# A nested seven-product scheme for the fourth product of stage one's first pair of steps, with a new order of stage one and S3 formed from S2

## The chip, the cores and the metric

The kernel runs on one core of one Trainium2 chip. The metric is the device time of one execution in microseconds; 904.12 us before the change, the median of three runs (904.05 to 904.26). The profile is that of one further execution.

## The reference

All data are fp32. An attention without softmax feeds a two-layer network:

```python
kv  = einsum('bhsd,bhse->bhde', k, v)      # 8 batches, 8 heads, 576 positions, head size 64
o   = einsum('bhsd,bhde->bhse', q, kv)
o   = o / sqrt(mean(o*o, -1) + 1e-6) * g_norm
x   = o with the heads side by side        # 4608 x 512
h   = x @ w_in                             # 512 x 2048
g   = s * relu(h)**2 + b
out = g @ w_out                            # 2048 x 512
```

## The kernel before

**Units and steps.** The 4608 rows of x are worked off in nine units (u = 0 to 8) of 512 rows. Each unit has a stage one (x times w_in, then relu, square and the affine of ScalarE) and a stage two (g times w_out). While unit u runs, the attention of unit u + 1 is done beside it, in two halves A and B: turn (VectorE L540, a transpose of q), product (TensorE L552), back (VectorE L564), square, row_sum (VectorE L575), norm (VectorE L585), turn_x (VectorE L592), scale. The k^T v products of the batches to come are kv (TensorE L384; ScalarE copies the result out at L400, into bd_kv).

**The seven-product scheme.** With C = A B in 2 x 2 blocks, seven products of half size take the place of eight: sums S1 to S4 of the one operand's blocks, sums T1 to T4 of the other's, products 1 to 7 of these, and sums of the products. Unit 0 is plain, unit 1 uses the scheme once, and units 2 to 8 use it on two levels: some of the seven products are themselves done by the scheme, with products of a quarter of their size.

**Stage one of units 2 to 8** (`mm1_deep`, L803 to L994). The 2048 columns of h are taken in four steps s = 0 to 3; steps 0 and 1 are pair 0, steps 2 and 3 pair 1. Here w_in is the operand A and x the operand B. Per step, products 1, 6, 5, 7 and 4 are whole products: `x1`, `x6`, `x5`, `y7`, `y4`, each a call of `mm1_product` with matmuls of 128x128 by 128x256. The function `y4(s)` multiplies A22 and T4 and adds the result to `r2`, kept in SBUF by `x6`. Products 2 and 3 go on by the scheme, for the two steps of a pair together: `small(i, pair, ...)` issues, for i = 2 or 3, small products 1 to 7 of 128x128 by 128x128 (four matmuls each), with their sums (`keep`, `add_relu`) on VectorE. The banks of PSUM for small are sx_ps (tag x of pool `ps_a`) for the small products 1, 6, 5 and 3, and z_ps (a single bank) for 2, 7 and 4. Of the sums of w_in that small needs, those of products 2 and 3 for both pairs (`DEEP`) are made once in unit 1 by `sums_of_w_in` and stored in DRAM (`w1_dram`) on the queue of POOL (GpSimd). SP loads them, like the parts of w_out, into a ring of NR = 14 slots (`pump` L1026), and a slot is freed by `used`. The sums of x for small are made by `sums_of_x` in `sub` tiles (six of them). Blocks of g are a11, a12, a21, a22 for each step, and s1 = a21 + a22; `done` does the square (L910) and the affine (L651) on ScalarE.

**Stage two of units 2 to 8** (`mm2`, `at_two_levels` L1110, `rest` L1368). g is A, w_out is B. All seven products go by the scheme, product 2 and 5 as one group, 7 and 3 as another. `do_25(6)` issues small product 6 of products 2 and 5; `go_73(1)` small product 1 of products 7 and 3, and `sums_...` forms the small sums of g on VectorE. S2, S3 and S4 of g are formed in place: `s2` writes S2 = S1 - A11 over a11, `s4` writes S4 = A12 - S2 over a12, and `s3` writes S3 = A11 - A21 over a21. Product 7 takes S3 as its operand. S3 of steps 0 and 1 is formed in stage one, the one just ahead of at(16), the other behind x5(3); S3 of steps 2 and 3 is formed in stage two, right after do_25(2) and at(1), by `step["s3"]`, before `s2` has overwritten a11.

**What sets the order.** The order is written out by hand: each engine carries out its own instructions in the order in which the functions are called, and there is no scheduler. In stage one `at(n)` calls the attention steps that `sides` (L1687) lists for the place n; stage two has places of its own. The lists for units 3 to 7 are the same but for kv, which stands at at(4) (at at(2) in unit 6) and is due in units 1 to 6; unit 2 has a list of its own, and unit 8 has none. The loads of q (L1624) and the stores of the output (L1211) go out on POOL's queue.

Of the kernel before, what the change touches and what calls it, by code (L numbers as in the profile page):

```python
# [10 lines left out]
FP32 = mybir.dt.float32  # L11
# [6 lines left out]
def kernel(  # L18
# [39 lines left out]
    nc = tc.nc  # L58
# [200 lines left out]
    def add(o, a, b):  # L259
        nc.vector.tensor_tensor(out=o, in0=a, in1=b, op=ALU.add)  # L260
# [53 lines left out]
    DEEP = ((2, 0), (3, 0), (2, 1), (3, 1))  # L314
# [464 lines left out]
    def sums_of_w_in(key, tags):  # L779

        i, pair = key
        w = [
            (ws[s][:, 2] if i == 3 else wa[s][:, KH:])
            for s in (2 * pair, 2 * pair + 1)
        ]
        a11, a12, a21, a22 = w[0][:, 0], w[0][:, 1], w[1][:, 0], w[1][:, 1]
        t = [
            xp.tile([P, KH, TB], FP32, name=f"xs_{n}", tag=f"xs_{n}").rearrange(
                "p k (b n) -> p (k b) n", n=P
            )  # L790
            for n in tags
        ]
        (s2, s3), (s1, s4) = ((x[:, :2], x[:, 2:]) for x in t)
        add(s1, a21, a22)
        sub(s2, s1, a11)
        sub(s3, a11, a21)
        sub(s4, a12, s2)
        for n in range(2):
            nc.gpsimd.dma_start(
                out=w1_dram[key][:, n], in_=t[n].rearrange("p f n -> p (f n)")  # L800
            )

    def mm1_deep(u):  # L803
# [4 lines left out]
        def sums_of_x():  # L808
            k0, k1 = (
                xT[u][:, KH + k].rearrange("p (g q c) -> p q g c", g=2, q=2) for k in range(2)  # L810
            )
            b11, b12, b21, b22 = k0[:, 0], k0[:, 1], k1[:, 0], k1[:, 1]
            t = [
                late["sub"].tile([P, FC // 4, P], FP32, name="sub", tag="sub", bufs=6) for _ in range(2)
            ]
            (t1, t2), (t3, t4) = ((x[:, :2], x[:, 2:]) for x in t)
            sub(t1, b12, b11)
            sub(t2, b22, t1)
            sub(t3, b22, b12)
            sub(t4, b21, t2)  # L820
            a.update({1: b11, 2: b21, 3: b22, 4: t4, 5: t1, 6: t2, 7: t3})
# [18 lines left out]

        def a22(s):
            t = g_tile("a22", s)
            add_relu(t, st["y", s], ga["a21", s])
# [10 lines left out]
        def s3(s):  # L854
            sub(ga["a21", s], ga["a11", s], ga["a21", s])

        def small(i, pair, *ms):
            name = {2: "a11", 3: "a21"}[i]

            def to(j, h):  # L860
                return g_pair[name, pair][:, j, :, h * P : h * P + P]

            def w_of(m):
                s0, s1 = 2 * pair, 2 * pair + 1
                raw = {1: (s0, 0), 2: (s0, 1), 4: (s1, 1)}
                if m in raw:
                    s, k = raw[m]
                    return ws[s][:, 2, k] if i == 3 else wa[s][:, KH + k]
                n, k = {6: (6, 0), 7: (6, 1), 5: (5, 0), 3: (5, 1)}[m]
                return ring[u, (i, pair), n][:, k]  # L870

            def keep(name, j, h):
                st[name] = late["tmp"].tile(
                    [P, 2, P], FP32, name="r", tag={"q2": "r2_2", "q4": "q4"}.get(name, "r14")
                )
                add(st[name], st["sx"], to(j, h))

            for m in ms:
                first = m in (1, 2, 7)
                if m == 1:  # L880
                    ps = ps_a.tile([P, DM], FP32, name="sx_ps", tag="x")
                    st["sx"] = ps.rearrange("p (b c) -> p b c", c=P)[:, :2]
                elif first:
                    ps = bank_of(("s", m), "z", 1).rearrange("p b (m c) -> p (b m) c", c=P)
                    st["sy"] = ps[:, :2]
                ps = st["sx" if m in (1, 6, 5, 3) else "sy"]
                w, x = w_of(m), a[m][:, i - 2]
                for b in range(2):
                    matmul(ps[:, b], w[:, b], x, first and b == 0, True)
                if m == 7:  # L890
                    used((u, (i, pair), 6))
                elif m == 3:
                    used((u, (i, pair), 5))
                if m == 1:
                    keep("q1", 0, 0)
                elif m == 2:
                    add_relu(to(0, 0), ps, st["q1"])
                elif m == 6:
                    keep("q2", 1, 0)
                elif m == 5:  # L900
                    keep("q4", 1, 1)
                    add_relu(to(1, 1), st["sy"], st["q4"])
                elif m == 3:
                    add_relu(to(0, 1), ps, to(0, 1))
                elif m == 4:
                    add_relu(to(1, 0), ps, st["q2"])
# [6 lines left out]
        def run(at, early):  # L913
# [6 lines left out]
            at(4)  # L920
            y7(0)
            small(2, 0, 6, 7)
            at(5)
            x5(0)
            small(2, 0, 5)
            a22(0)
            at(6)
            x6(1)
            done("a22", 0)
            small(2, 0, 3, 4)  # L930
            at(7)
            y4(0)
            at(8)
            y7(1)
            done("a11", 0, 1)
            at(9)
            x5(1)
            done("a12", 0)
            a22(1)
            at(10)  # L940
            x1(2)
            small(3, 0, 1, 2)
            at(11)
            x1(3)
            done("a22", 1)
            y4(1)
            at(12)
            small(3, 0, 6, 7)
            y7(2)
            at(13)  # L950
            small(3, 0, 5)
            x6(2)
            done("a12", 1)
            at(14)
            small(3, 0, 3, 4)
            x6(3)
            done("a21", 0)
            at(15)
            small(2, 1, 1, 2)
            x5(2)  # L960
            done("a21", 1)
            s1(0)
            s3(0)
            at(16)
            small(2, 1, 6, 7)
            a22(2)
            y7(3)
            done("a22", 2)
            s1(1)
            small(2, 1, 5)  # L970
            x5(3)
            s3(1)
            small(2, 1, 3, 4)
# [12 lines left out]
        def rest_of_3():  # L986
# [5 lines left out]
            s1=lambda: (s1(2), s1(3)), s3=lambda: (s3(2), s3(3)),  # L992
# [73 lines left out]
    def mm2(u, step=None, side={}):  # L1066
# [301 lines left out]
        def rest():  # L1368
# [21 lines left out]
            step["s3"]()  # L1390
# [21 lines left out]
            go_6(7)  # L1412
            do_6(5)
# [177 lines left out]
    def side_of(A, B, sums, u):  # L1591

        if u == 0:
# [9 lines left out]
        of_w_in = [  # L1603
            partial(sums_of_w_in, *with_tags)
            for with_tags in zip(DEEP, ((5, 6), (7, 4), (5, 6), (7, 4)))
        ]
# [5 lines left out]
            6: [B["norm"], of_w_in[1]],  # L1612
            8: [B["turn_x"], B["scale"], of_w_in[2]],
            9: [of_w_in[3]],
            11: [sums],
            13: [partial(loads, 3, 1)],
            3: [of_w_in[0]],
# [69 lines left out]
    def sides(u, A, B):  # L1687
# [9 lines left out]
        if u == 1:  # L1697
            for s in range(1, NS - 1):
                first[((0, 1), (0, 3))[s - 1]] = list(sums_w_in(s))
            first.update({  # L1700
                (1, 3): kv,
                (2, 0): [A["turn"]],
                (2, 1): [A["product"]],
                (2, 2): [A["back"]],
                (2, 3): [A["square"]],
                (3, 0): [A["row_sum"]],
                (3, 2): [A["norm"], A["turn_x"]],
                (3, 3): [lambda: [load() for load in load_q(12, rest_on=nc.sync)]],
            })
            return first, second  # L1710
        if u + 1 == U:
            return first, second
        if u == 2:
            first = {
                4: [A["turn"]],
                5: kv,
                8: [A["product"]],
                9: [A["back"], B["turn"]],
                10: [A["square"]],
                11: [A["row_sum"]],  # L1720
                12: [B["product"]],
                13: [A["norm"]],
                14: [A["turn_x"]],
                15: [B["back"], *q[0]],
            }
            second = {
                0: [B["square"]], 1: [B["row_sum"], A["scale"]], 2: [B["norm"]], 3: [B["turn_x"], *q[1]],
                "sums": [B["scale"]],
            }
        else:  # L1730
            first = {
                2: [A["turn"], *(kv if u == 6 else [])],
                4: [A["product"], *(kv if u != 6 else [])],
                5: [A["back"]],
                6: [A["square"], B["turn"]],
                7: [A["row_sum"]],
                8: [A["norm"]],
                9: [A["turn_x"]],
                10: [B["product"], *q[0]],
                11: [B["back"], A["scale"]],  # L1740
                12: [B["square"]],
                13: [B["row_sum"]],
                14: [B["norm"]],
                15: [B["turn_x"], *q[1]],
            }
            second = {1: [B["scale"]]}
# [101 lines left out]
```

## Time and profile before

| | |
|---|---|
| median of three runs | 904.12 us (904.05 to 904.26) |
| the profiled execution | 904.66 us |
| its span, from the first to the last instruction | 902.9 us |
| mean granted TensorE clock | 1.000 |
| instructions | 19433 |
| chain of work that ended last, by engine | PE 93%, VectorE 4%, DMA 1%, ScalarE 1% |
| the chain's largest lines | x_ps L92 46%, y_ps L92 28%, z_ps L92 10%, sx_ps L92 6% |
| starts of units 2, 3, 4, 5 (us) | 234.5, 332.2, 427.7, 523.6 |
| starts of units 6, 7, 8 (us) | 619.3, 715.2, 808.4 |

How to read it. Engines are PE (TensorE's matmuls), PEld (its weight loads, which overlap PE), DVE (VectorE), ACT (ScalarE), POOL (GpSimd), SP (SyncE, which issues loads). L92 is line 92 of the kernel; as all matmuls of this kind are issued by one helper there, and the additions and subtractions by the helpers at L260 and L263, they are told apart by their tiles: `z_ps<-sub,w_sb` is a matmul into the tile z_ps from the tiles sub and w_sb. A row of a timeline is the start in us from the beginning of the span, the length of the row in us, engine, line, operation, tiles, shapes, and the number of records that were drawn together (x8); in brackets stands the idle time of the engine just before it and what ended that. Matmuls are pipelined, so that rows of PE overlap, and the distance between two starts is the time that the first one took from the stream. A row of the waits is: the engine and the line that waited, the engine and the line that it waited for, then total us, number of times, and the longest.

### The profile page before, as it was taken

How to read it: one execution, taken by the hardware profiler on the slowest of the kernel's cores; microseconds unless marked ns; L12 is line 12 of the kernel's file. 1: busy time of each engine (PE TensorE's matmuls, PEld its weight loads, DVE VectorE, ACT ScalarE, POOL GpSimd, SP SyncE). 2: the span in 40 equal slices, each digit the busy share in tenths (PEclk: the TensorE clock that was granted, in tenths of full speed). 3: DMA queues.
4: the chain of work that ended last, by engine and by line, in shares of the span. 5: the costliest groups of instructions: out<-in, count | busy, mean ns of one | idle time of the engine just before them, and what ended most of it. 6: DMA issues, size and time to landing. Idle time of an engine off the chain costs nothing.

```text
span 902.9 us, 19433 instructions
## 1 busy us (share of the span) xinstructions
PE 891.4 (99%) x7578; PEld 822.1 (91%) x7578; DVE 658.2 (73%) x1240; ACT 347.0 (38%) x584; POOL 265.8 (29%) x501
## 2 busy tenths in 40 slices
PE   7999999999999999999999999999999999999998
PEld 6888888888889998999899988999899989999998
DVE  2898686687557975798668856885779767972696
ACT  2887023531157115720464026601670056204610
POOL 2027057014732333711373026503440300021000
PEclk9999999999999999999999999999999999999999
DMA  9897637249943994289527972599239812991286
GB/s 255 310 337 235 194 98 244 69 118 400 338 131 94 307 317 146 71 268 329 185 70 213 314 253 69 154 307 320 66 88 314 288 41 54 303 306 46 59 280 187
DMA packets 118987, 184.55 MB, mean 204 GB/s; under 512 B 25200, under 2 KB 42992, under 8 KB 118896
## 3 DMA queue, kind: packets, MB, share of 16 engines
q1 hardware_dynamic: 98288, 155.36, 54.0%
q0 software_dynamic: 17152, 25.72, 9.6%
q10 hardware_dynamic: 3456, 2.23, 1.0%
q8 instruction: 60, 0.98, 0.4%
q14 instruction: 31, 0.25, 0.1%
HBM read 157.03 MB, written 26.21 MB: 203 GB/s over the span
## 4 chain that ended last, share of the span: by engine, by line
PE 93%; DVE 4%; DMA 1%; ACT 1%; issue 0%; ACTq 0%; DVEq 0%
PE x_ps L92 46%; PE y_ps L92 28%; PE z_ps L92 10%; PE sx_ps L92 6%; PE y_ps L552 2%; DMA kv_sb<-in_v_dram 1%; PE kv_ps L384 1%; PE z_ps L384 1%; DVE a L263 0%; DVE xn L585 0%; PE y_ps L384 0%; DVE sub L263 0%; DVE xT L596 0%; DVE o L260 0%; DVE xs L263 0%
## 5 line engine op out<-in xcount | busy, mean ns | idle before, releaser
L1624 POOL DMA_DIRECT2D q_sb<-in_q_dram x312 | 175.8, 572 | 136.5 <-ACT a L910 76.2
L92 PE MATMUL x_ps<-w_sb,sub 128*128 128x128 f32 x1176 | 148.8, 275 | 1.1 <-DVE r L260 1.1
L1211 POOL DMA_DIRECT2D out_dram<-o x120 | 59.4, 502 | 303.8 <-issue 151.1
L92 PEld LDWEIGHTS x_ps<-w_sb,sub 128*128 128x128 f32 x1176 | 139.7, 192 | 1.5 <-DVE r L260 1.5
L651 ACT ACTIVATE a<-a,b_col,s_col 128x512 f32<-128x512 f32 x144 | 117.0, 813 | 26.1 <-DVE a L654 17.8
L92 PE MATMUL y_ps<-xs,wb 128*128 128x256 f32 x528 | 124.6, 381 | 0.0
L92 PEld LDWEIGHTS y_ps<-xs,wb 128*128 128x128 f32 x528 | 97.0, 190 | 12.9 <-issue 1.0
L826 ACT COPY a<-x_ps 128x512 f32<-128x512 f32 x28 | 16.3, 583 | 220.1 <-PE x_ps L92 220.1
L260 DVE TENSOR_TENSOR r<-sx_ps,a 128x256 f32<-128x256 f32 x84 | 35.4, 422 | 79.3 <-PE sx_ps L92 79.3
L92 PE MATMUL x_ps<-xs,ws_raw 128*128 128x256 f32 x384 | 91.2, 380 | 0.1
L92 PE MATMUL x_ps<-xT,wa 128*128 128x256 f32 x360 | 83.9, 381 | 0.1
L92 PEld LDWEIGHTS x_ps<-xs,ws_raw 128*128 128x128 f32 x384 | 70.0, 190 | 8.7 <-ACT r L725 0.5
L910 ACT ACTIVATE a<-a 128x512 f32<-128x512 f32 x112 | 69.8, 623 | 18.4 <-DVE a L267 18.4
L92 PEld LDWEIGHTS x_ps<-xT,wa 128*128 128x128 f32 x360 | 66.7, 190 | 10.4 <-issue 1.5
L92 PE MATMUL x_ps<-w_sb,a 128*128 128x128 f32 (+1 forms) x432 | 64.9, 298 | 0.0
L92 PE MATMUL y_ps<-w_sb,a 128*128 128x128 f32 (+1 forms) x416 | 62.1, 295 | 0.0
L92 PEld LDWEIGHTS x_ps<-w_sb,a 128*128 128x128 f32 x432 | 58.4, 192 | 2.9 <-issue 0.4
L92 PEld LDWEIGHTS y_ps<-w_sb,a 128*128 128x128 f32 x416 | 56.1, 192 | 2.1
L92 PE MATMUL y_ps<-w_sb,sub 128*128 128x128 f32 x392 | 49.5, 275 | 0.0
L260 DVE TENSOR_TENSOR r<-x_ps,o 128x256 f32<-128x256 f32 (+1 forms) x84 | 29.7, 353 | 26.7 <-PE x_ps L92 26.0
L263 DVE TENSOR_TENSOR a<-a,a 128x512 f32<-128x512 f32 x72 | 46.8, 684 | 0.4
L92 PE MATMUL z_ps<-w_sb,a 128*128 128x128 f32 (+1 forms) x352 | 46.9, 280 | 0.0
(207 smaller groups left out, 1512.1 us busy)
## 6 DMA issues: line engine op xcount, KB each, us to landing
w_sb<-w SPq DMA_DIRECT2D x399, 256.0 KB, 5.1
w_sb<-w SPq DMA_DIRECT2D x14, 512.0 KB, 8.8
w<-sub POOLq DMA_DIRECT2D x28, 256.0 KB, 6.6
out_dram<-o POOLq DMA_DIRECT2D x112, 64.0 KB, 4.1
w_sb<-in_k_dram SPq DMA_DIRECT2D x24, 288.0 KB, 4.8
w_sb<-in_v_dram SPq DMA_DIRECT2D x24, 288.0 KB, 5.0
w_raw<-in_moe_w_in_dram SPq DMA_DIRECT2D x6, 1024.0 KB, 8.1
q_sb<-in_q_dram POOLq DMA_DIRECT2D x160, 32.0 KB, 2.9
```

Source lines behind the costliest of these rows:

```text
L92: nc.tensor.matmul(o, lhsT=lhsT, rhs=rhs, start=start, stop=stop, skip_group_check=True)
L260: nc.vector.tensor_tensor(out=o, in0=a, in1=b, op=ALU.add)
L263: nc.vector.tensor_tensor(out=o, in0=a, in1=b, op=ALU.subtract)
L384: nc.tensor.matmul(ps[r][(r ^ l) * HB : (r ^ l) * HB + HB, i, :], lhsT=kv[l][0][rows, j, :], rhs=kv[l][1][rows, j, :], start=(j == 0), sto ...
L552: nc.tensor.matmul(ps[l][32 * p : 32 * p + 32, r, lo:hi], lhsT=bd_kv[b % 2][rows, p, at : at + 32], rhs=st["qT"][rows, p, lo:hi], start=Tr ...
L651: nc.scalar.activation(t, t, AF.Identity, scale=s_col, bias=b_col)
L826: nc.scalar.copy(g_tile("a11", s), st["x", s])
L910: nc.scalar.square(ga[name, s], ga[name, s])
L1211: queues[s % 2].dma_start(out=view[b, jj, :, cols], in_=st[name, j][s * w : s * w + w, cols])
L1624: load()
```

## The change

From unit 2 on, product 4 (A22 times T4) of steps 0 and 1 goes by the scheme too: `small(4, 0, ...)`, seven small products for the pair, takes the place of y4(0) and y4(1). Its result is accumulated in g's tile of a12, and `a12(s)` is y7's result plus r2 put there ahead of it, on VectorE. The sums of T4 are formed by `sums_of_x4` in one more `sub` tile (four subtractions of 128x128). The sums of w_in for the key (4, 0) are made, stored and loaded as for the others: two stores more in unit 1, and two loads of 256 KB more per unit. All these sums are now made in unit 1's stage one (before: in the stage two of that unit), in halves, in `sub` tiles.

As small(4, 0) and small(3, 0) run interleaved, as do small(3, 0) and small(2, 1), small(3, 0) gets banks of its own, from the pool `ps_t` (tag t, the one that the attention's transposes and products use), and tiles q1t, q2t, q4t of its own.

The order of stage one is new from the first y7 to the last x5. Among other things, small(2, 0, 6, 7) now stands ahead of y7(0) and right behind at(4) and at(5), and the places at(5) to at(16) lie elsewhere in the stream. The attention steps of `sides` are moved with it; in unit 2, whose attention ran into stage two, square and row_sum of B and scale of A are now in stage one.

S3 is now formed for all four steps at one place of stage two: after s4, do_6(2, 6) and go_6(7), and before do_6(5) and go_73(1), as a22 - a11, where a11 holds S2 by then.

```diff
-    DEEP = ((2, 0), (3, 0), (2, 1), (3, 1))
+    DEEP = ((2, 0), (4, 0), (3, 0), (2, 1), (3, 1))
...
-    def sums_of_w_in(key, tags):
+    def sums_of_w_in(key):
...
-        add(s1, a21, a22)
-        sub(s2, s1, a11)
-        sub(s3, a11, a21)
-        sub(s4, a12, s2)
-        for n in range(2):
-            nc.gpsimd.dma_start(
-                out=w1_dram[key][:, n], in_=t[n].rearrange("p f n -> p (f n)")
-            )
+        t = {}
+
+        def part(n, *steps):
+            x = late["sub"].tile([P, FC // 4, P], FP32, name="sub", tag="sub", bufs=6)
+            t[n] = x[:, :2], x[:, 2:]
+            for step in steps:
+                step()
+            nc.gpsimd.dma_start(
+                out=w1_dram[key][:, n], in_=x.rearrange("p f n -> p (f n)")
+            )
+
+        return (
+            lambda: part(0, lambda: sub(t[0][1], a11, a21), lambda: sub(t[0][0], a22, t[0][1])),
+            lambda: part(1, lambda: add(t[1][0], a21, a22), lambda: sub(t[1][1], a12, t[0][0])),
+        )
...
+        def sums_of_x4():
+            x = xs[u, 4]
+            b11, b12, b21, b22 = (x[:, k, q * P : q * P + P] for k in range(2) for q in range(2))
+            t = late["sub"].tile([P, FC // 4, P], FP32, name="sub", tag="sub", bufs=6)
+            t1, t2, t3, t4 = (t[:, n] for n in range(4))
+            sub(t1, b12, b11)
+            sub(t2, b22, t1)
+            sub(t3, b22, b12)
+            sub(t4, b21, t2)
...
+        def a12(s):
+            add(g_tile("a12", s), st["y", s], st["r2", s])
...
         def s3(s):
-            sub(ga["a21", s], ga["a11", s], ga["a21", s])
+            sub(ga["a21", s], ga["a22", s], ga["a11", s])
...
-            name = {2: "a11", 3: "a21"}[i]
+            name = {2: "a11", 3: "a21", 4: "a12"}[i]
+            g = (i, pair)
+            apart = g == (3, 0)
...
+            def bank_for(m):
+                if apart:
+                    ps = ps_t.tile([P, 2, 2 * P], FP32, name="st_ps", tag="t")
+                    return ps[:, 0].rearrange("p (b c) -> p b c", c=P)
+                if m == 1:
+                    ps = ps_a.tile([P, DM], FP32, name="sx_ps", tag="x")
+                    return ps.rearrange("p (b c) -> p b c", c=P)[:, :2]
+                ps = bank_of(("s", m), "z", 1).rearrange("p b (m c) -> p (b m) c", c=P)
+                return ps[:, :2]
```

The order in `run`, before and after (the calls of done left out, all others in their order):

```diff
-x1(0) at(2) x1(1) sums_of_x small(2,0,1,2) x6(0) at(4) y7(0) small(2,0,6,7) at(5)
-x5(0) small(2,0,5) a22(0) at(6) x6(1) small(2,0,3,4) at(7) y4(0) at(8) y7(1) at(9)
-x5(1) a22(1) at(10) x1(2) small(3,0,1,2) at(11) x1(3) y4(1) at(12)
-small(3,0,6,7) y7(2) at(13) small(3,0,5) x6(2) at(14) small(3,0,3,4) x6(3) at(15)
-small(2,1,1,2) x5(2) s1(0) s3(0) at(16) small(2,1,6,7) a22(2) y7(3) s1(1)
-small(2,1,5) x5(3) s3(1) small(2,1,3,4) a22(3) early at(18) y4(2) ...
+x1(0) at(2) x1(1) sums_of_x small(2,0,1,2) x6(0) at(4) at(5) small(2,0,6,7) y7(0) at(6)
+small(2,0,5) a12(0) x6(1) at(7) small(2,0,3,4) y7(1) sums_of_x4 a12(1) x5(0)
+small(4,0,1,2) a22(0) at(8) x5(1) small(4,0,6,7) at(9) a22(1) at(10) x1(2) at(11)
+small(4,0,5) x1(3) at(12) small(4,0,3,4) x6(2) at(13) small(3,0,1,2) y7(2) at(14)
+small(3,0,6,7) small(2,1,1,2) x6(3) at(15) small(3,0,5) small(2,1,6,7) x5(2)
+small(3,0,3,4) small(2,1,5) a22(2) y7(3) small(2,1,3,4) at(16) x5(3) s1(0) s1(1)
+a22(3) early at(18) y4(2) ...
```

Stage two, and the attention steps:

```diff
             do_25(2)
             at(1)
-            step["s3"]()
             s2((0,))
...
             s4((1, 2, 3))
             go_6(7)
+            step["s3"]()
             do_6(5)
             sums_73((5, 6), 7)
             sums_73((), 3)
             go_73(1)
...
         if u == 2:
-            first:  4 A.turn; 5 kv; 8 A.product; 9 A.back, B.turn; 10 A.square; 11 A.row_sum;
-                    12 B.product; 13 A.norm; 14 A.turn_x; 15 B.back, q[0]
-            second: 0 B.square; 1 B.row_sum, A.scale; 2 B.norm; 3 B.turn_x, q[1]; "sums" B.scale
+            first:  4 A.turn; 6 kv; 7 A.product; 8 A.back, A.square, B.turn; 9 A.row_sum;
+                    10 B.product; 11 B.back; 12 A.norm; 13 A.turn_x, q[0]; 14 B.square;
+                    15 B.row_sum; 16 A.scale
+            second: 1 B.norm; 2 B.turn_x; 3 q[1]; "sums" B.scale
         else:
-            first:  2 A.turn (kv, u == 6); 4 A.product (kv, u != 6); 5 A.back; 6 A.square, B.turn;
-                    7 A.row_sum; 8 A.norm; 9 A.turn_x; 10 B.product, q[0]; 11 B.back, A.scale;
-                    12 B.square; 13 B.row_sum; 14 B.norm; 15 B.turn_x, q[1]
+            first:  2 A.turn (kv, u == 5); 4 A.product (kv, u != 5); 5 A.back, A.square, B.turn;
+                    6 A.row_sum; 7 A.norm; 8 A.turn_x; 10 B.product, q[0];
+                    11 B.back, B.square, A.scale; 12 B.row_sum; 13 B.norm; 14 B.turn_x; 15 q[1]
```

In unit 1 the stage-two list loses its four calls of sums_of_w_in (places 3, 6, 8, 9), and the stage-one list gains ten halves, spread over the places (1, 0) to (3, 0) between the attention steps.

## The prediction, on record before the changed kernel ran

> **What bounds the kernel now.** I read the page first, then TensorE's waits, then the timelines of TensorE and VectorE (DVE) around the places that the diff touches. Units are counted from 0; unit 2 is the third.
>
> ```profile
> PE 891.4 (99%) x7578; PEld 822.1 (91%) x7578; DVE 658.2 (73%) x1240; ACT 347.0 (38%) x584; POOL 265.8 (29%) x501
> ```
>
> The waits of TensorE (engine, line, whom it waited for: total us, times, longest) hold only seven rows. Six belong to the start; the one below is all that it waits in the steady part:
>
> ```profile
> PE x_ps L92 <- DVE r L260: 1.1, 2, 0.7
> ```
>
> So TensorE is back to back: a microsecond taken out of its stream is gained, and a microsecond by which any operand is late is lost in full. Two shapes fill the stream. TensorE, end of unit 4's stage one (start, us, shape, records):
>
> ```profile
> 475.71 1.89 PE L92 MATMUL y_ps<-xs,wb 128*128 128x256 f32 x8
> 477.44 0.61 PE L92 MATMUL sx_ps<-sub,w_sb 128*128 128x128 f32 x4
> 477.88 0.61 PE L92 MATMUL z_ps<-sub,w_sb 128*128 128x128 f32 x4
> ```
>
> The cost is the distance between starts, as matmuls overlap: y4 takes 477.44 - 475.71 = 1.73 us, one product of small takes 0.445 (a pair of them, 381.74 to 382.63 in unit 3, 0.89).
>
> **Term 1, the scheme applied to A22 T4.** Per unit two y4 (3.46) go and seven products of small (3.115) come: -0.345, over seven units -2.4 us. VectorE gets seven more instructions of 0.42 us and four subtractions of 128x128 (0.29) per unit; in stage one it waits 6.9 us at once in unit 4 (before 439.75) and some 0.5 to 2.3 us a dozen times more, so this lies beside the matmuls. ScalarE's work is the same. SP gets two more loads of 256 KB per unit; no row of TensorE's waits names such a load, they land 5.1 us after issue, and 14 slots run ahead. Without that cover each late load would cost up to those 5 us.
> [...] The trace has 0.111 us per record against 0.216, nearly half, and it decides.
>
> **Term 2, S3 later.** Before, S3 of steps 2 and 3 is formed after do_25(2), those of steps 0 and 1 in stage one. Now all four stand on VectorE after S4 and ahead of the output of do_6(5), and go_73(1), two products later on TensorE, reads S3 of steps 0 and 1 as weights. The built order confirms it: its third call waits for the second S3. The same place now, TensorE and then VectorE:
>
> ```profile
> 405.41 1.06 PE L92 MATMUL y_ps<-w_sb,sub 128*128 128x128 f32 x8
> 406.30 1.06 PE L92 MATMUL x_ps<-w_sb,sub 128*128 128x128 f32 x8
> 407.19 1.95 PE L92 MATMUL x_ps<-w_sb,a 128*128 128x128 f32 x16
> ...
> 414.34 1.95 PE L92 MATMUL y_ps<-w_sb,sub 128*128 128x128 f32 x16
> ```
>
> ```profile
> 394.86 1.28 DVE L263 TENSOR_TENSOR a<-a,a 128x512 f32<-128x512 f32 x2
> ...
> 405.61 0.29 DVE L260 TENSOR_TENSOR r<-x_ps,o 128x128 f32<-128x128 f32 x1 [0.53 <-PE x_ps L92]
> 405.81 1.89 DVE L263 TENSOR_TENSOR a<-a,a 128x512 f32<-128x512 f32 x3
> 407.62 0.28 DVE L260 TENSOR_TENSOR r<-x_ps,o 128x128 f32<-128x128 f32 x1
> ...
> 413.10 1.28 DVE L263 TENSOR_TENSOR sub<-a 128x512 f32<-128x512 f32 x2
> ```
>
> At 405.61 VectorE has been waiting for TensorE (0.53), so work taken away earlier (the two at 394.86) cannot bring it forward. From there it is without a gap until 413.10. Three S4 start at 405.81, 0.603 apart, so S3 start at 407.62, 408.22, 408.82 and 409.42, each 0.684 long. go_73(1) starts at 407.19 now. How a wait ends is seen in unit 2: VectorE's row at 300.51 lasts 0.42, TensorE resumes at 300.98, 0.05 after it, and its 16 records take 1.89 instead of 1.79:
>
> ```profile
> 300.98 2.05 PE L92 MATMUL x_ps<-w_sb,sub 128*128 128x128 f32 x16 [0.74 <-DVE r L260]
> ```
>
> So a wait costs its length plus 0.10. The second S3 ends at 408.90; the third call runs at 408.90 + 0.05 + 0.10 = 409.05 instead of 407.64: 1.42 late. VectorE's queue behind is moved by 4 x 0.603 = 2.41: the output of do_6(5), two sums for product 7, r1, outputs, and the first subtraction at 413.10, which go_73(7) reads (414.34 now). It ends at 413.78 + 2.41 = 416.19; TensorE, 1.42 late, would be there at 415.76 and starts at 416.34: 0.58 more. After that VectorE now has a wait of 1.95 us (at 418.11) and catches up. Together 2.0 us per unit. The rows repeat within 0.02 us in units 3 to 8: 6 x 2.0 = 12.0. Nothing hides it. Bounds: the first wait alone, 8.5; all of the 2.41 of the queue, 14.5.
>
> **Term 3, stage two of unit 2.** Its two waits (0.74 and 0.35, with what follows 1.5 us) come from attention steps on VectorE. One step, row_sum (1.13), moves to stage one and two S3 (1.2) leave, which removes both. But norm and turn_x still stand there, so VectorE reaches do_6(6) some 0.65 late (0.4 on TensorE), and the two S3 waits then cost about 1.6 and 0.5. Net +1.0, bounds 0 and 2.
>
> **Term 4, stage one of units 3 to 7.** small(2, 0, 6, 7) now follows kv or the attention product directly, where y7 (1.73 us) stood between. In units 3, 4 and 6 its seventh product takes the z bank, which ScalarE still copies after kv:
>
> ```profile
> 437.31 0.53 ACT L400 COPY bd_kv<-z_ps 64x128 f32<-64x128 f32 x2 [2.71 <-PE y_ps L384]
> ```
>
> The copies end at 437.84; the product would start 0.445 after 437.21, at 437.66: with 0.05 and 0.10 it is 0.33 late. In units 5 and 7 there is no kv between, and VectorE has back (1.2) and B's turn (1.16), both moved up, ahead of the addition that frees the bank for product 5: 0.4 late. Sum 3 x 0.33 + 2 x 0.4 = 1.8, bounds 0 (if the banks are free in time) and 3.5 (0.7 each, the length of the whole addition more).
>
> **Term 5, stage one of unit 2.** B's product, moved from at(12) to at(10), now comes 22.5 us after the unit's start (three x1-size products sooner), and its operand, B's turn, follows a22(0) and back on VectorE: those end at about 22.2, turn takes 1.24. Wait 1.1. Now B's turn waits for its load:
>
> ```profile
> 259.45 1.25 DVE L540 STREAM_TRANSPOSE qT<-q_sb 128x1024 f32<-128x1024 f32 x1 [4.58 <-DMA q_sb<-in_q_dram]
> ```
>
> If the load lands as late as now (25 us after the start), the wait is 3.9. But POOL's queue has eight stores fewer ahead of it in stage two of unit 1, and VectorE's waits of 1.2 and 0.4 for such stores go, so I take it 3 to 5 us sooner, and 1.1 for the term; bounds 0 and 4.
>
> The sums of w_in themselves move to stage one of unit 1: twenty VectorE instructions (8 us) into waits that sum to over 13 us there (5.6 before 156.82 the longest), ten stores behind POOL's loads of q, which end at 158.2. Zero; without that cover 1.5, the largest gap between what stands at one place and its idle time. The new banks of small(3, 0) are those of attention's products, which are read before: zero.
>
> **Sum.** -2.4 + 12.0 + 1.0 + 1.8 + 1.1 = +13.5 us. The profiled execution took 904.66 (span 902.9), so 918.2 for one like it; the median of the runs shown is 0.54 lower: **917.6**.
>
> **Rivals.**
> A, the queue of VectorE recovers: only the first wait of term 2 (8.5) and little of terms 3 to 5: +6 to +10, about 912. For it: the second wait is a margin of 0.58. Against it: VectorE shows no gap between 405.61 and 413.10.
> B, S3 in time: VectorE reaches S3 at least 1.3 us sooner than TensorE needs it, and the saving alone stays: 904.1 - 2.4 = 901.7, faster. It decides if all waits together stay under 2.4 us, 0.35 per unit. For it: VectorE is busy 73% only, and S3 was taken out of two earlier places. Against it: the 0.53 us of idle time ahead of the row at 405.61.
> C, unit 2's load late (term 5 at 4) and term 2 at its upper end: above 921, about 923.
> That the change does not do what it says is excluded by the built order.
>
> **Chances.** Forecast (914 to 921) 0.58; A 0.18; C 0.13; B 0.08; a sum between B and A 0.03, of which 0.02 within 0.2%, about what a measurement of this kernel tells from no change. Range 910 to 923: A's and the forecast's times and half of C. Faster 0.08, same 0.02, slower 0.90.
>
> **What will show it.** Right: TensorE's waits name DVE a L263 some 1.3 us long once per unit, sub L263 some 0.5 us once per unit; periods of units grow by about 2 us; blocks of y4 at 1.73 give way to seven of 0.445. Wrong: no wait of TensorE at go_73(1), or records of small further apart than 0.111 us.

## The result, and the profile after

The changed kernel took 918.95 us (median of four runs, 918.86 to 921.89), the kernel before 904.19 (904.05 to 905.81) beside it: a ratio of 1.0167, 95% interval 1.0144 to 1.0190. Predicted were 917.6 within 910 to 923. The profiled execution is the one of 921.89; another one, traced later, took 919.93.

The busy times of the changed kernel, from its page:

```profile
PE 897.6 (98%) x7662; PEld 827.2 (90%) x7662; DVE 684.2 (74%) x1321; ACT 345.2 (38%) x584; POOL 266.6 (29%) x503
```

TensorE shows 84 matmul records more and is busy for 6.2 us more than before, but the span has grown by 17.2 (920.1 against 902.9). The rest shows as waiting; the busy time too holds some loss, as rows overlap and short waits hide in them. TensorE's waits in it (the engine waited, for whom: total us, times, longest), without the six rows of the start:

```profile
PE x_ps L92 <- issue: 7.6, 7, 1.3
PE y_ps L552 <- DVE qT L540: 2.2, 1, 2.2
...
PE y_ps L92 <- DVE sub L263: 1.4, 7, 0.2
...
PE x_ps L92 <- ACT r L725: 1.3, 1, 1.3
```

The rows with "issue" and with DVE sub occur seven times: once in each unit from 2 to 8. The other two are single waits, in unit 2 (for DVE qT) and in unit 1 (for ACT r).

Where a stage begins and ends can be read from the starts of TensorE's first product of each stage. The lengths of the stages (us), from three traces; that of unit 8's stage two is taken to its last matmul, and the other stages differ by less than 0.1:

| unit, stage | before | changed, first trace | changed, second trace |
|---|---|---|---|
| 1, one | 49.12 | 50.59 (+1.47) | 51.47 (+2.35) |
| 2, one | 50.84 | 54.42 (+3.58) | 51.74 (+0.90) |
| 2, two | 46.86 | 47.77 (+0.91) | 47.80 (+0.94) |
| 3, one | 50.42 | 50.34 (-0.08) | 50.33 (-0.09) |
| 4, one | 50.58 | 50.50 (-0.08) | 50.50 (-0.08) |
| 5, one | 50.48 | 50.70 (+0.22) | 50.70 (+0.22) |
| 6, one | 50.88 | 50.50 (-0.38) | 50.50 (-0.38) |
| 7, one | 48.14 | 48.16 (+0.02) | 48.15 (+0.01) |
| 8, one | 45.69 | 45.37 (-0.32) | 45.38 (-0.31) |
| 3 to 8, two, each | 45.01 to 45.12 | +1.94 to +1.95 | +1.94 to +1.97 |

So 11.7 of the 17.2 us lie in stage two of units 3 to 8, the same in each; units 1 and 2 hold 6.0 in the first trace and 4.2 in the second. (In unit 5 and unit 6 the list of places moves kv between at(2) and at(4), in opposite ways; only the sum of the two, -0.16, says something of the change.)

The place of the loss in unit 3, TensorE and then VectorE:

```profile
412.24 1.06 PE L92 MATMUL x_ps<-w_sb,sub 128*128 128x128 f32 x8
414.34 2.16 PE L92 MATMUL x_ps<-w_sb,a 128*128 128x128 f32 x16 [1.04 <-issue]
416.34 1.12 PE L92 MATMUL x_ps<-w_sb,sub 128*128 128x128 f32 x8
...
419.97 1.95 PE L92 MATMUL x_ps<-w_sb,sub 128*128 128x128 f32 x16
422.12 2.05 PE L92 MATMUL y_ps<-w_sb,sub 128*128 128x128 f32 x16 [0.20 <-DVE sub L263]
```

```profile
411.54 0.29 DVE L260 TENSOR_TENSOR r<-x_ps,o 128x128 f32<-128x128 f32 x1 [0.56 <-PE x_ps L92]
411.75 4.29 DVE L263 TENSOR_TENSOR a<-a,a 128x512 f32<-128x512 f32 x7
415.96 0.28 DVE L260 TENSOR_TENSOR r<-x_ps,o 128x128 f32<-128x128 f32 x1
...
421.39 1.28 DVE L263 TENSOR_TENSOR sub<-a 128x512 f32<-128x512 f32 x2
```

The seven subtractions at 411.75 are three S4 and four S3, 0.603 apart: the first S3 starts at 411.75 + 3 x 0.603 = 413.56 and ends 0.68 later, at 414.24. TensorE is done with do_6(5) at 412.24 + 0.89 = 413.13 and starts go_73(1) at 414.34: 1.21 late, and its 16 records take 2.00 instead of 1.79. That is 1.42 in all. The profile names "issue" here, not VectorE; that the wait is for S3 shows from the time, and from the runs below in which S3 stands elsewhere. go_73(7) would start at 419.97 + 1.79 = 421.76; its operand, the first subtraction at 421.39, ends at 422.07, it starts at 422.12 and is slower by 0.10: 0.46. Together 1.88 of the 1.94.

### The profile page after: what moved, and what is told of

It is laid out like the page before. It is cut to its first block, busy times and chain, and to the rows that moved or that the text cites. A ratio compares the mean times of both kernels' runs of the same rounds, so it can differ in the third digit from the quotient of the medians.

```text
span 920.1 us, 19738 instructions
## 1 busy us (share of the span) xinstructions
PE 897.6 (98%) x7662; PEld 827.2 (90%) x7662; DVE 684.2 (74%) x1321; ACT 345.2 (38%) x584; POOL 266.6 (29%) x503
## 4 chain that ended last, share of the span: by engine, by line
PE 81%; DVE 13%; DMA 4%; ACT 1%; issue 1%; ACTq 0%; DVEq 0%; SPq 0%; POOLq 0%
PE x_ps L92 39%; PE y_ps L92 22%; PE z_ps L92 8%; PE sx_ps L92 5%; DVE a L263 4%; PE st_ps L92 2%; DVE sub L263 2%; DVE o L260 2%; PE y_ps L552 2%; DMA w_sb<-w 1%; DVE sub L260 1%; DMA kv_sb<-in_v_dram 1%; DVE r L260 1%; PE kv_ps L384 1%; PE z_ps L384 1%
## 5 line engine op out<-in xcount | busy, mean ns | idle before, releaser
L92 PE MATMUL y_ps<-xs,wb 128*128 128x256 f32 x416 | 98.5, 380 | 0.0
L92 PE MATMUL x_ps<-xT,wa 128*128 128x256 f32 x360 | 85.8, 387 | 0.1
L92 PEld LDWEIGHTS y_ps<-xs,wb 128*128 128x128 f32 x416 | 76.3, 190 | 9.1 <-issue 0.2
L92 PEld LDWEIGHTS y_ps<-w_sb,sub 128*128 128x128 f32 x392 | 46.5, 192 | 2.7 <-DVE sub L263 2.7
```

Source lines behind the costliest of these rows:

```text
L92: nc.tensor.matmul(o, lhsT=lhsT, rhs=rhs, start=start, stop=stop, skip_group_check=True)
```

## The experiments

**S3 back at its old place, all four.** Edit: in the changed kernel, S3 as a11 - a21 again, and

```diff
             at(1)
+            step["s3"]()
             s2((0,))
...
             go_6(7)
-            step["s3"]()
```

> The changed kernel with all four S3 formed right after do_25(2) and at(1), as a11 - a21, ahead of s2; all else as changed. Theory (S3 stands too late on VectorE, and nothing else makes stage two longer): TensorE's two waits per unit vanish, stage two of units 3 to 8 goes from 47.06 back to 45.1 to 45.2 us, and the time from 918.95 to about 906 (7 x 1.9 less). Rival (VectorE's queue in stage two is full, so that four S3, 4 x 0.60 us where two stood before, are late or make others late wherever they stand): the waits move to another product, stage two stays above 46.3, the time above 911.

Measured: 915.67 us (913.35 to 917.41) against 905.01, ratio 1.0119 (1.0101 to 1.0138). Stage two of units 3 to 8 took 46.25, 1.13 more than before and 0.81 less than in the changed kernel. The waits at go_73 are gone, and a new one is there, in unit 3 this, TensorE and then VectorE:

```profile
397.93 1.95 PE L92 MATMUL y_ps<-w_sb,sub 128*128 128x128 f32 x16
400.69 1.49 PE L92 MATMUL x_ps<-w_sb,sub 128*128 128x128 f32 x11 [0.81 <-DVE r L260]
```

```profile
397.21 2.49 DVE L263 TENSOR_TENSOR a<-a,a 128x512 f32<-128x512 f32 x4
399.62 0.68 DVE L263 TENSOR_TENSOR a<-s,a 128x512 f32<-128x512 f32 x1
400.22 0.42 DVE L260 TENSOR_TENSOR r<-x_ps,o 128x256 f32<-128x256 f32 x1
```

Four S3 and an S2 now stand ahead of the addition at 400.22, which reads the bank that do_25(5) writes into. The rival was nearer: four S3 in a row do not fit here either.

**S3 split between the stages.** Edit to the kernel of the run before: s3(0) and s3(1) behind s1(1) in stage one, only steps 2 and 3 in stage two.

> As the run before, but S3 of steps 0 and 1 is formed at the end of stage one, right after s1(1), and only steps 2 and 3 after do_25(2), as in the kernel before. Theory: 905.5 to 906.5, stage two at 45.1 in units 3 to 8, stage one as in the changed kernel (50.3 to 50.7 in units 3 to 6). Rival (VectorE full in stage two): 1.2 us less per unit than with all four S3 in stage two, at least 7 us less than that run.

Measured: 907.82 us (905.77 to 910.31) against 905.01, above the 905.5 to 906.5 expected; stage two of units 3 to 8 at 45.00 to 45.12, as in the kernel before, and neither row of seven waits is left. Stage one is as in the changed kernel. What remains over the kernel before is in unit 1 (+1.30) and unit 2 (+3.43; in this trace too TensorE waits 2.1 us for B's turn, and x1(2) behind it takes 3.51 us, 261.56 to 265.07, instead of 1.73). The place of S3 is the whole loss of stage two in these units; at the old place there is room for two S3, not for four.

**The late S3 alone, in the kernel before.**

```diff
-            sub(ga["a21", s], ga["a11", s], ga["a21", s])
+            sub(ga["a21", s], ga["a22", s], ga["a11", s])
...
-            s3(0)
...
-            s3(1)
...
             go_6(7)
+            step["s3"]()
             do_6(5)
```

> The kernel before with one part of the change alone: all four S3 as a22 - a11 after go_6(7). Theory: stage two of units 3 to 8 grows by 1.9 us each as in the changed kernel, unit 2's by 1.5 to 2.5; 904.2 + 13 = about 917, between 916 and 918.5; TensorE shows a wait of about 1 us before go_73(1) and 0.2 before go_73(7) in every unit. Rival (the stall needs the new order of stage one or the additional VectorE work to come about): under 910.

Measured: 917.95 us (917.38 to 918.18) against 905.01, ratio 1.0145 (1.0130 to 1.0160), +12.9 us. Stage two of units 3 to 8 grew by 1.94 to 1.96 and unit 2's by 1.24 (1.5 to 2.5 expected), with the same two rows of waits:

```profile
PE x_ps L92 <- issue: 7.6, 7, 1.3
...
PE y_ps L92 <- DVE sub L263: 1.4, 7, 0.2
```

This one edit brings 12.9 us, against 14.8 for the whole change, without the new order and without the scheme.

**Product 4 as whole products again**, in the changed kernel: y4(0) and y4(1) in the places of small(4, 0, 6, 7) and small(4, 0, 3, 4); a12, sums_of_x4 and the loads for them are left out (the sums of w_in for them are still made in unit 1).

> The changed kernel with y4(0) and y4(1) as whole products in the places of small(4, 0, 6, 7) and small(4, 0, 3, 4); a12, sums_of_x4 and the loads of key (4, 0) are left out, the order of all else is kept. Theory (28 records of 0.111 us stand against 16 of 0.216): stage one grows by 0.3 to 0.35 us per unit, in all +2.4 us, about 921.3. [...]

Measured: 924.40 us (923.20 to 925.53), where 921.3 was expected. Unit by unit, stage one is longer than in the changed kernel by 0.32, 0.33, 0.33, 0.34 and 0.33 us in units 3, 4, 5, 7 and 8, and by 0.49 in unit 2; in unit 6 it is 0.91, with a pause of 0.5 us inside kv that no other trace shows. (The profiled spans are 922.5 and 920.1. The median lies 5.5 above that of the changed kernel, but in another series, where the kernel before took 905.01, and with units 1 and 2 in it, which vary between executions; so the stages are compared.) So the scheme saves what 28 records of 0.111 us against 16 of 0.216 say, 0.33 per unit.

**The sums of w_in one place later in unit 1**, on top of the split S3: halves 6 to 9 move from the places (2, 1) to (3, 0) to (2, 2) to (3, 1).

> As the run with S3 split between the stages; besides, the last four of the ten halves of the sums of w_in stand one place later in unit 1's stage one each, so that the seventh half is formed some 2 us later. Theory (unit 1 grew because VectorE waits for a sub tile whose store stands on POOL's queue behind the loads of q, and then ScalarE's copy and TensorE come late): VectorE's wait of 2.6 us for a store shrinks to under 1, TensorE's wait for the copy r goes, stage one of unit 1 falls from 50.4 to 49.1 to 49.5 us. Rival (twenty more VectorE instructions in unit 1 make it late wherever they stand): it stays at 50.0 or more. All else as in the run with S3 split, so about 1 us less.

Measured: 905.51 us (904.56 to 907.36) against 904.67, ratio 1.0010 (1.0001 to 1.0019); stage one of unit 1 at 49.03, 0.09 below the kernel before, and VectorE's wait for a store and TensorE's wait for the copy r are gone. What was wrong there is seen in the changed kernel, VectorE, POOL and TensorE:

```profile
165.51 0.43 DVE L263 TENSOR_TENSOR sub<-wa,wa 128x256 f32<-128x256 f32 x1 [2.63 <-DMA w<-sub]
```

```profile
152.74 5.17 POOL L1653 DMA_DIRECT2D q_sb<-in_q_dram  x9 [1.51 <-issue]
159.06 0.58 POOL L1653 DMA_DIRECT2D q_sb<-in_q_dram  x1 [1.14 <-DMA q_sb<-in_q_dram]
159.95 0.58 POOL L794 DMA_DIRECT2D w<-sub  x1 [0.31 <-DMA w_sb<-w]
```

```profile
169.09 1.99 PE L92 MATMUL x_ps<-xs,ws_raw 128*128 128x256 f32 x8 [1.28 <-ACT r L725]
```

The first store of these sums stands behind loads of q and goes out at 159.95; the seventh half takes the tile that it reads (there are six), so VectorE stands until 165.51; ScalarE's next copy and TensorE follow late.

**B's product later in unit 2**, on top of that: from at(10) to at(12), A's norm ahead of it, B's back at at(13).

> As the run before; besides, in unit 2 B's product moves from at(10) to at(12), behind x1(2), small(4, 0, 5) and x1(3), and A's norm ahead of it; B's back follows at at(13). Theory (TensorE waits for B's turn, 2.1 us, and the clock drop that follows costs another 1.8): both go, stage one of unit 2 falls from 54.3 to 50.6 to 51.0, and the time is about 902.5, below the kernel before. Rival (the load of q arrives later still, and the wait only moves with it): a wait for DVE qT of 1 us or more stays, stage one above 51.8.

Measured: 904.16 us (903.84 to 905.03) against 904.67, ratio 0.9995 (0.9986 to 1.0004), not the 902.5 expected. TensorE no longer waits for B's turn, but stage one of unit 2 took 51.39: part of the wait moved, to small(4, 0, 5), whose bank VectorE reads only after B's turn:

```profile
259.94 0.71 PE L92 MATMUL sx_ps<-sub,w_sb 128*128 128x128 f32 x4 [0.57 <-DVE r L260]
```

**y7(0) ahead of small(2, 0, 6, 7) again**, on top of that.

> As the run before; besides, y7(0) stands again between at(4) and small(2, 0, 6, 7), as in the kernel before. Theory (in units 3, 4 and 6 the z bank, in units 5 and 7 the sx bank come free too late for small(2, 0, 6, 7)): stage one falls by 0.2 to 0.4 us in each of the units 3 to 7, to what the kernel before took less 0.33 (50.1 in unit 3, 47.8 in unit 7), in all 1 to 2 us less than the run before: about 901.5, 2.3 to 3 below the kernel before. Rival (other costs of the new order, such as where at(10) and at(11) stand, make up the difference to the pure saving): less than 0.1 per unit.

Measured: 905.48 us (905.02 to 905.96) against 904.67, ratio 1.0007 (0.9998 to 1.0016), 1.3 more than the run before: a miss. Stage one grew by 0.40 even in unit 8, which has neither kv nor attention. Unit 8, TensorE and then VectorE:

```profile
816.33 0.61 PE L92 MATMUL sx_ps<-sub,w_sb 128*128 128x128 f32 x4
816.78 0.61 PE L92 MATMUL z_ps<-sub,w_sb 128*128 128x128 f32 x4
817.53 0.71 PE L92 MATMUL sx_ps<-sub,w_sb 128*128 128x128 f32 x4
```

```profile
817.05 0.42 DVE L260 TENSOR_TENSOR r<-sx_ps,a 128x256 f32<-128x256 f32 x1 [3.36 <-PE sx_ps L92]
```

Small product 5 writes on into the bank that VectorE still reads for product 6 (817.05 to 817.47); it would start at 816.78 + 0.445 = 817.23 and starts at 817.53. With y7(0) gone from between 7 and 5, nothing covers this read. In the changed kernel y7(0) covers it, and leaves the z bank's copy uncovered; one product cannot stand in both places.

**A whole product in each of the two places**, and B's turn in unit 2 at at(10), on top of that; the order of this part against that of the changed kernel:

```diff
             at(4)
+            y7(0)
             at(5)
             small(2, 0, 6, 7)
-            y7(0)
             at(6)
+            x6(1)
             small(2, 0, 5)
             a12(0)
-            x6(1)
             at(7)
-            small(2, 0, 3, 4)
             y7(1)
+            small(2, 0, 3, 4)
```

> As the run with y7(0) first; besides, x6(1) stands between small(2, 0, 6, 7) and small(2, 0, 5), and y7(1) between small(2, 0, 5) and small(2, 0, 3, 4), so that every two small products on one bank have a whole product between them; in unit 2, B's turn moves from at(8) to at(10), behind a22(1). Theory (the run before lost because small(2, 0, 5) followed small(2, 0, 7) directly, while VectorE still read the bank sx): the 0.40 us in units 3 to 8 go, and so do the waits for the z bank and for product 5 that were left: stage one at 50.1 in unit 3, 47.8 in unit 7, 45.4 in unit 8; in unit 2 the 0.7 us ahead of small(4, 0, 5) goes, 50.6. About 902.0, 2.6 us below the kernel before. Rival (the saving of 0.33 per unit is used up by the additional VectorE work whatever the order): 904 or more.

Measured: 903.04 us (902.59 to 903.69) against 905.40, ratio 0.9975 (0.9966 to 0.9985): the first version whose interval lies wholly below the kernel before. Stage one is 50.09, 50.31, 50.35, 50.26, 47.82 and 45.37 in units 3 to 8, as expected; together that is 2.0 below the kernel before, 6 times the 0.33 of the scheme, so the additional work of VectorE need not use the saving up. In unit 2 it is 51.25, not 50.6: 0.63 us of waiting now stand ahead of small(4, 0, 3), since A's norm was put before the addition that frees its bank.

**Two S3 late instead of four**, on top of the kernel with B's product later: S3 of steps 2 and 3 after go_6(7).

> The run with unit 2 later (S3 split, y7 not moved), but S3 of steps 2 and 3 formed as a22 - a11 after go_6(7), those of steps 0 and 1 still in stage one. TensorE's go_73(1) does not read steps 2 and 3. Theory A (two causes: the operand of go_73(1) itself, and VectorE's queue being pushed back, for what go_73(7) reads): no wait before go_73(1), but half of the push, 1.2 us, reaches go_73(7), which waits 0.6 to 0.9; stage two of units 3 to 8 at 45.7 to 46.0. Theory B (only the operand counts): stage two stays at 45.1.

Measured: 909.31 us in one run; stage two of units 3 to 8 at 45.75 to 45.87, +0.74 to +0.76, as theory A has it. go_73(1) starts without a wait at 407.73 in unit 3; go_73(7) waits:

```profile
406.83 1.06 PE L92 MATMUL x_ps<-w_sb,sub 128*128 128x128 f32 x8
407.73 1.95 PE L92 MATMUL x_ps<-w_sb,a 128*128 128x128 f32 x16
409.69 1.16 PE L92 MATMUL x_ps<-w_sb,sub 128*128 128x128 f32 x8
...
413.37 1.95 PE L92 MATMUL x_ps<-w_sb,sub 128*128 128x128 f32 x16
415.52 2.05 PE L92 MATMUL y_ps<-w_sb,sub 128*128 128x128 f32 x16 [0.20 <-DVE sub L263]
```

The wait there is 0.46 again (415.52 - 413.37 - 1.79 + 0.10), and do_6(3) adds the rest: it starts at 409.69 instead of 407.73 + 1.79 = 409.52 and takes 0.11 longer than 0.89, in all 0.28. So the queue of VectorE is a second cause beside the operand.

**The changed kernel once more.**

> The changed kernel once more, unaltered, for a second trace: the profiled execution took 921.89 us, the other three 918.86 to 919.04. Theory (the 3 us are unit 2's stage one, where the wait for B's turn was 2.2 us and a stretch of 3.4 us at half the clock followed): in an execution near 918.9, stage one of unit 2 takes 51.5 to 52.3 us instead of 54.42, without the stretch at half the clock, and every other stage is as in the first trace within 0.4. Rival: the difference is spread over the stages. If the clock falls again, the execution takes about 921 to 922 and this tells nothing new.

Measured: 919.93 us. The column "second trace" of the table above is this run. Stage one of unit 2 took 51.74 and the clock stayed at 1.00, as the theory has it; unit 1 took 0.88 more than in the first trace (TensorE's wait for the copy r was 2.2 us instead of 1.3), which it had not expected.

## Why the prediction was right, point by point

**Term 1, the saving** (predicted -0.345 per unit, -2.4): -0.32 in unit 8, the only one without attention, and 0.33 by the run that undoes it: -2.3.

**Term 2, late S3** (2.0 per unit, +12.0): 1.94 per unit, +11.7. The first wait is 1.42, to the hundredth what was worked out; the second is 0.46 instead of 0.58. In one detail the prediction was off: TensorE stands before the first call, for the first S3 (1.21), and then is slower over the group (0.21), instead of standing 1.42 before the third call. That the sum agrees is no luck: the second S3 ends at 411.75 + 4 x 0.603 + 0.68 = 414.84, and in the trace the fifth record of go_73(1), the first of its third call, starts at 414.90, so the second S3 sets the end as predicted. The sign that was named, a wait for "DVE a L263" in the list, did not come: the profile put these waits down to "issue". Rival A (VectorE catches up) falls with it, and so does rival B (S3 in time).

**Term 3, stage two of unit 2** (+1.0): +0.91 and +0.94. The two old waits for r are gone from the list, and go_73(1) and go_73(7) lose 1.67 and 0.46 there (1.6 and 0.5 predicted).

**Term 4, stage one of units 3 to 7** (+1.8): mechanism right, sizes a little too large. With the saving of 0.33 taken off, units 3 and 4 lose 0.25 each (0.33 predicted), units 5 and 6 together 0.50 (0.73), unit 7 0.35 (0.40): 1.35. Both waits are where they were placed: in unit 3 ScalarE's copy from the z bank, 347.80 to 348.33, and the product behind it at 348.39; in unit 7 VectorE's addition from the sx bank, 738.23 to 738.62, and product 5 behind it at 738.67.

**Term 5, stage one of unit 2** (wait 1.1, with the saving +0.75): +0.90 in the second trace, where B's turn (259.41) follows back without waiting for its load and TensorE waits 1.22. In the first trace the load is later: VectorE waits 1.13 for it, TensorE 2.20, and the clock drop below comes on top, +3.58. The prediction had this wait in its rival C, but not the clock.

**Unit 1, priced at zero**: this is the step that failed. "ten stores behind POOL's loads of q" was named, and 1.5 "without that cover", and then the waits of VectorE were taken as the cover. They cover the instructions, not the store: the half that needed a tile whose store was still queued stopped VectorE (for 2.63 us in the first trace), however much idle time it had later. It cost 1.47 and 2.35, the latter more than the 1.5 too.

**The sum**: predicted +13.5 for one execution; +17.2 in the first trace, of which unit 1 is 1.5 and the late load with the clock drop 2.7; +15.3 in the second. The median grew by 14.8. In the second trace unit 1 adds 2.35, and the other terms together come to 0.5 less than predicted, which takes part of it back. The predicted median is 1.4 below the measured one; as no execution at the median was traced, how this 1.4 is made up is not shown.

## What to carry to other kernels

Where one engine is busy without a gap, an operation on another engine is placed by the queue ahead of it and by what stands behind it, not by that engine's total share: VectorE at 73% had room for two S3 at the old place of stage two and not for four, and not even for two behind S4. Two small products on one bank needed work between them to cover the read of the bank (0.42 us in unit 8; without it the second started 0.30 late); when a filler is moved, look at both pairs that it separated. A `sub` tile that was stored to DRAM came free for VectorE 5.56 us after the issue of its store (159.95 to 165.51), and that store stood behind the loads of q on POOL's queue, the last one ahead of it at 159.06; so look at what stands ahead of a store, not only at the idle time of the engine that fills the tile.

## What the runs showed of the hardware

In the first trace of the changed kernel the granted clock of TensorE fell behind a wait. Four stretches of that trace (from and to, length, then busy us of PE, PEld, DVE, ACT and POOL with the number of instructions, the granted clock, DMA share, GB/s):

```profile
255.20:258.60 3.40, 3.40 (x25) 3.19 (x23) 2.67 (x5) 3.21 (x6) 0.00 (x0) 1.00 0.59 194
258.60:262.00 3.40, 1.20 (x34) 0.50 (x32) 2.31 (x3) 1.53 (x3) 0.00 (x0) 1.00 0.27 80
262.00:265.40 3.40, 3.40 (x16) 2.73 (x9) 2.19 (x4) 1.64 (x3) 0.00 (x0) 0.52 0.00 0
265.40:268.80 3.40, 3.40 (x22) 3.10 (x22) 2.55 (x5) 1.48 (x3) 0.00 (x0) 0.98 0.00 0
```

In the second stretch TensorE was busy for 1.20 of 3.40 us, and in the next 3.4 us the granted clock was 0.52; x1(2) took 3.52 us (262.02 to 265.54) instead of 1.73, so that 1.79 us came on top of the wait of 2.20. In the second trace the wait at this place was 1.22, and two stretches there read:

```profile
258.10:261.50 3.40, 2.19 (x43) 1.65 (x41) 3.26 (x5) 2.71 (x4) 0.00 (x0) 1.00 0.29 75
261.50:264.90 3.40, 3.40 (x33) 2.85 (x18) 3.06 (x6) 2.20 (x4) 0.00 (x0) 1.00 0.08 28
```

Here the clock stayed at 1.00.

A like loss stands at this place in two other traces: with S3 split, after a wait of 2.07, x1(2) took 3.51 us; with product 4 as whole products, after a wait of 2.44, the attention product took 1.89 us (260.74 to 262.63) instead of the 1.03 of the changed kernel. The mean granted clock of these three executions is 0.998. The length of the wait alone does not decide: the second trace also has a wait of 2.2 us in unit 1 (TensorE for the copy r), and the run with all four S3 at the old place one of 2.2 us in unit 2's stage two, with a mean granted clock of 1.000 and 0.999. What decides is not shown by these runs.

Beside that, the profile put seven waits of about 1.1 us each down to "issue", where the times and the runs that move S3 point to VectorE.
